# Exchanging four quadrants' maxima by transfers within SBUF instead of a small matrix product

## The chip, the cores and the metric

The kernel runs on one core of a Trainium2 chip. The metric is the device time of one execution, in microseconds (us); less is better. The time before is 823.92 us, the median of three runs.

## The reference

Two attention steps share one set of 32 inducing points, and a maxout layer follows:

```python
B, N, m, C = (4, 12544, 32, 128)      # scale = 1 / sqrt(C)

def mab(q, kv):
    s = scale * (q @ kv.transpose(0, 2, 1))
    s = s - s.max(-1, keepdims=True)
    a = np.exp(s)
    a /= a.sum(-1, keepdims=True) + 1e-09
    return a @ kv
h = mab(I, x)            # 32 inducing points attend to 12544 tokens
out = mab(x, h)          # each token attends to the 32 results

h = np.maximum(np.maximum(x @ w1, x @ w2), x @ w3)   # x: out, 50176 x 128; 768 wide
return h @ w_out
```

All of it is in float32. The softmax of the first step runs over all tokens of a batch, so a maximum over 12544 scores is needed for each of the 32 inducing points; the kernel keeps a running one and rescales.

## The kernel before

**Tiling.** A batch has 98 tiles of 128 tokens. They form seven groups: group 0 with two tiles, groups 1 to 6 with 16. A group of 16 tiles is cut into four chunks of 512 tokens, group 0 is one chunk of 256; that makes 25 chunks in a batch and 100 in all. The 768 hidden columns are six pieces of 128.

**Two phases at once.** Phase 1 of a batch is the first attention, inducing points over tokens. Phase 2 is the second attention and the maxout layer for every token, and is most of the work. Phase 1 of batch 0 runs alone at the start (`phase1_first`). Phase 1 of batches 1 to 3 is woven into phase 2 of the batch before.

**Slots.** Phase 2 is a list of 600 slots, one for each chunk and piece. `advance` issues for slot s: the product pu of the next slot (line 669), pv of this one (675), the relu ru of pu on ScalarE (684), the high part hi of the slot before (691, ScalarE), its low part lo (699 on GpSimd, or 705 on VectorE), and the maximum h of pv and ru on VectorE (702). Six slots later `stage2` multiplies hi and lo by w_out into acc (727 to 729; line 726 once in a chunk). The banks of pu, pv and acc come in pairs, so pu of slot s+2 waits until ru of slot s has read its bank, and pv of slot s+2 waits for h of slot s. `finish` copies a chunk's acc on ScalarE and stores it through SyncE's queue (744, 745).

**The order is written out by hand** for all five engines: each engine runs its instructions in the order in which the code issues them. `main` goes through the slots and, after `advance`, calls what the table `plan` holds for that slot; `at(s, f, ...)` enters a call. A window is 24 slots, one group of 16 tiles; its first slot is s0. Bursts of products for phase 1 and for the scores of phase 2 stand at s0 + 2 and s0 + 15.

**The softmax of phase 1 for one group** (`softmax1`), where the change lies. `attend_products` (282) writes the scores to a PSUM bank in four quadrants: partition 32 q + m holds inducing point m over quarter q of the group's tokens. So a maximum along a partition is that of one quarter only, and the four quadrants must be joined:

- `attend_max` (292, VectorE): the negative maximum mq of each partition.
- `attend_column` (299, ScalarE): md, mq put in the column of its quadrant of four columns.
- `attend_spread` (306, TensorE): a product of md with the constant sel, which gives every partition the values of all four quadrants of its inducing point.
- `attend_least` (312, or 315 and 316, VectorE): the least of the four, and of the running one in the batch's later groups, into mneg.
- `attend_weights` (322, ScalarE): the exponential a with that bias, and its sums. `attend_scale` (365): the factor al for the groups before.
- `attend_transpose` (336, VectorE), then in a later burst `attend_sums` (346, TensorE) and `attend_add` (382).

The argument `wait` of `softmax1` delays the steps after md; for groups 2 and 3 of a batch it is LATE.

**SyncE's queue (SP)** issues nearly all transfers, in program order: for each chunk four copies within SBUF that lay out its probabilities pT (654), 32 partitions each; the output stores; for each group two loads of 1 MB, the tokens xg (100, `load_tokens`) and the channels xT (111, `load_channels`); and at a batch's end 16 copies for its weights us (570). An instruction of SP that waits holds back all behind it. A transfer also waits until the eighth transfer before it has landed, because eight semaphores are used in turn.

Of the kernel before, what the change touches and what calls it, by code (L numbers as in the profile page):

```python
# [8 lines left out]
F32 = mybir.dt.float32  # L9
# [4 lines left out]
ALU = mybir.AluOpType  # L14
AX = mybir.AxisListType
# [10 lines left out]
def kernel(ctx, tc, x, xt, ind_t, w1, w2, w3, w_out, out):  # L26
    nc = tc.nc
    B, N, C = x.shape
    M = ind_t.shape[1]
    DF = w1.shape[1]  # L30
    P = 128
    NT = N // P
    NJ = DF // P
    NQ = P // M
# [18 lines left out]
    ORDER = "a a a a b a a b 0 c d m b a b a b a p d b 1 c s b b b s S m b q 2 c s 3 c s d s s d s"  # L53
    STEPS2 = (3, 5, 7, 8, 9, 10, 11, 13, 14, 15)
    scale = 1.0 / float(C) ** 0.5
    LATE = 12
    LOWVEC = (23, 0, 15, 18)
    LOWLAST = (23, 0, 9, 15, 18)
    UW = 2 * DF + C
# [5 lines left out]
    while t0 < NT:  # L65
        nt = NT % GT if t0 == 0 and NT % GT else GT
        assert nt == GT or nt <= NQ
        g = dict(t0=t0, nt=nt, at=t0 * P)
        groups.append(g)
        t0 += nt  # L70
    NG = len(groups)

    const = ctx.enter_context(tc.tile_pool(name="const", bufs=1))
    xp = ctx.enter_context(tc.tile_pool(name="xp", bufs=2))
    xtp = ctx.enter_context(tc.tile_pool(name="xtp", bufs=7))
    wk = ctx.enter_context(tc.tile_pool(name="wk", bufs=2))
    bp = ctx.enter_context(tc.tile_pool(name="bp", bufs=2))
    hp = ctx.enter_context(tc.tile_pool(name="hp"))
    op = ctx.enter_context(tc.tile_pool(name="op", bufs=2))
# [45 lines left out]
    def first_loads():  # L125
# [13 lines left out]
        out=sel[:, :M], in_=ident.rearrange("p (q m) -> p m q", m=M), axis=AX.X, op=ALU.add  # L139
    )  # L140
    nc.vector.tensor_copy(
        out=sel[:, M:].rearrange("p (q m) -> p q m", m=M),
        in_=sel[:, :M].unsqueeze(1).to_broadcast([P, NQ - 1, M]),
# [94 lines left out]
    state = {}  # L238

    def start_batch(b):  # L240
        st = state[b] = {"xT": {}, "xg": {}, "a": {}, "s": {}}
        st["mneg"] = bp.tile([P, NG], F32, name="mneg", tag="mneg")
        st["lst"] = bp.tile([P, NG], F32, name="lst", tag="lst")
        if b == 0:
            st["hg"] = const.tile([P, NG, C], F32, name="hg")
        else:
            st["hs"] = bp.tile([P, C], F32, name="hs", tag="hs")
# [39 lines left out]
    def attend_max(b, gi):  # L287

        w = groups[gi]["nt"] * M
        st = state[b]  # L290
        mq = wk.tile([P, 1], F32, name="mq", tag="mq")
        nc.vector.tensor_reduce(out=mq, in_=st["a"][gi][:, :w], axis=AX.X, op=ALU.max, negate=True)
        st["mq"] = mq

# [13 lines left out]
    def attend_least(b, gi):  # L308
        st = state[b]
        new, mp = st["mneg"][:, gi : gi + 1], st["mp"]  # L310
        if b == 0 or gi == 0:
            nc.vector.tensor_reduce(out=new, in_=mp[:, :NQ], axis=AX.X, op=ALU.min)
        else:

            nc.vector.tensor_reduce(out=mp[:, NQ : NQ + 1], in_=mp[:, :NQ], axis=AX.X, op=ALU.min)
            nc.vector.tensor_tensor(out=new, in0=mp[:, NQ : NQ + 1], in1=st["mneg"][:, gi - 1 : gi], op=ALU.min)

    def attend_weights(b, gi):
        w = groups[gi]["nt"] * M
        st = state[b]  # L320
        a = wk.tile([P, 512], F32, name="a", tag="a")
        nc.scalar.activation(
            out=a[:, :w],
            in_=st["a"][gi][:, :w],
            func=AF.Exp,
            bias=st["mneg"][:, gi : gi + 1],
            accum_out=st["lst"][:, gi : gi + 1],
        )
        st["a"][gi] = a
# [32 lines left out]
    def attend_scale(b, gi):  # L362
        st = state[b]
        st["al"] = wk.tile([P, 1], F32, name="al", tag="al")
        nc.scalar.activation(
            out=st["al"],
            in_=st["mneg"][:, gi - 1 : gi],
            func=AF.Exp,
            bias=st["mneg"][:, gi : gi + 1],
            scale=-1.0,  # L370
        )

# [25 lines left out]
    def phase1_first():  # L398
# [19 lines left out]
        half(1, 0)  # L418
        attend_spread(0, bank_o[0])
        attend_least(0, 0)  # L420
        half(1, 8)
        work(WORK[0])
# [347 lines left out]
    def at(s, f, *args):  # L770
        plan[s].append((f, args))

    def softmax2(b, gi, *when):

        gen = []

        def step():
            if not gen:
                gen.append(scores_steps(b, gi))
            next(gen[0], None)  # L780

        for s in when:
            at(s, step)

    def softmax1(b, gi, s, wait=0):

        at(s + 2, attend_max, b, gi)
        at(s + 3, attend_column, b)
        at(s + 6 + wait, attend_spread, b)
        at(s + 7 + wait, attend_least, b, gi)  # L790
        at(s + 8 + wait, attend_weights, b, gi)
        if gi > 0:
            at(s + 9 + wait, attend_scale, b, gi)
        at(s + 10 + wait, attend_transpose, b, gi)

    def burst(s, *what):

        for f, *args in what:
            at(s, f, *args)

    for b in range(B):
        base = b * per_batch + short
        n = b + 1
        for g in range(1, NG):
            s0 = base + (g - 1) * WIN
            first, second = [], []
            if g + 1 < NG:

                if n == B:

                    if g % 2:
                        first += [(scores_products, b, k, bank_a[k % 2]) for k in (g + 1, g + 2) if k < NG]
                elif b > 0 or g > 1:
                    first.append((scores_products, b, g + 1, bank_a[0]))
                softmax2(b, g + 1, *(s0 + i for i in STEPS2))
            if n < B:

                if g == 1:
                    if n == 1:
                        at(s0 + 1, load_tokens, 1, 4)  # L820
                    at(s0 + 4, load_channels, n, 2)
                    first.append((attend_products, n, 0, bank_a[1]))
                    softmax1(n, 0, s0 + 2)
                    second += [(attend_products, n, 1, bank_a[1]), (attend_sums, n, 0)]
                    at(s0 + 16, attend_add, n, 0)
                    softmax1(n, 1, s0 + 15)
                    at(s0 + 16, load_tokens, n + 1, 0)
                    at(s0 + 20, load_channels, n, 3)
                elif g < NG - 2:
                    first += [(attend_products, n, g, bank_a[1]), (attend_sums, n, g - 1)]  # L830
                    at(s0 + 3, attend_add, n, g - 1)
                    softmax1(n, g, s0 + 2, 0 if g == NG - 3 else LATE)
                    at(s0 + 4, load_channels, n, g + 2)
                    more = g + 3
                    if more < NG:
                        at(s0 + 5, load_tokens, n, more)
                    else:
                        at(s0 + 5, load_tokens, n + 1, more - NG + 1)
                    if g == NG - 3:
                        second += [(attend_products, n, g + 1, bank_a[1]), (attend_sums, n, g)]  # L840
                        at(s0 + 16, attend_add, n, g)
                        softmax1(n, g + 1, s0 + 15)
                        at(s0 + 16, load_tokens, n + 1, 2)
                elif g == NG - 2:
                    first += [(attend_products, n, g + 1, bank_a[1]), (attend_sums, n, g)]
                    at(s0 + 3, attend_add, n, g)
                    softmax1(n, g + 1, s0 + 2)
                    at(s0 + 5, load_tokens, n + 1, 3)
                    second.append((attend_sums, n, g + 1))
                    at(s0 + 16, load_tokens, n + 1, 4)  # L850
                    at(s0 + 16, attend_add, n, g + 1)
                    at(s0 + 18, add_quadrants, ("state", n), bank_a[1])
                    at(s0 + 18, total_sums, ("state", n), bank_a[0])
                    at(s0 + 19, invert_total, ("state", n))
                    at(s0 + 19, combine_states, ("state", n), 1)
                    at(s0 + 21, combine_products, ("state", n), bank_a[0])
                    at(s0 + 22, combine_high, ("state", n))
                    at(s0 + 23, combine_low, ("state", n))
                    for r in range(NQ):
                        at(s0 + 25 + 3 * r, combine_rows, ("state", n), r)  # L860
                else:
                    first += [(scores_products, n, 1, bank_a[0]), (scores_products, n, 0, bank_a[1])]
                    softmax2(n, 1, *(s0 + i for i in STEPS2))
                    softmax2(n, 0, *(s0 + i for i in (4, 6, 8, 9, 10, 11, 12, 13, 14, 15)))
                    if n + 1 < B:
                        at(s0 + 18, start_batch, n + 1)
                        at(s0 + 18, load_channels, n + 1, 0)
                        at(s0 + 18, load_channels, n + 1, 1)
            burst(s0 + 2, *first)
            burst(s0 + 15, *second)  # L870
# [25 lines left out]
    with tc.manual_schedule(engines=MANUAL):  # L896
        phase1_first()
        st = state[0]
# [9 lines left out]
        for step in ORDER.split():  # L908
# [10 lines left out]
            elif step == "m":  # L919
                more = len(st["up"])  # L920
# [67 lines left out]
```

## Time and profile before

| what | value |
|---|---|
| runs | 823.32, 823.92, 826.77 us; median 823.92 us |
| span of the profiled execution | 821.3 us; the median lies 2.6 us above it |
| busy: TensorE, ScalarE, GpSimd, VectorE | 98%, 91%, 79%, 76% |
| granted clock of TensorE | 1.000 over the span |
| DMA | 102.51 MB, mean 125 GB/s |

A row of a group of instructions reads: line of the kernel, engine, operation, output <- inputs, shapes, number of instructions, then busy time and mean length. A row of a timeline reads: start, length, engine, line, operation, number, and in brackets the engine's idle time before it with what ended that. PE is TensorE, DVE is VectorE, ACT is ScalarE, SPq is SyncE's queue. A matmul of float32 data takes two passes, each with a record of its own (the spread: 56 records for 28 products). Matmuls overlap, so the distance between starts tells what one costs.

### The profile page before, as it was taken

Reading aid. Unit: us, or ns where it says so; the run is one execution under the profiler, and the core shown is the slowest. Engines: PE = TensorE matmul, PEld = TensorE weight load, DVE = VectorE, ACT = ScalarE, POOL = GpSimd, SP = SyncE. Lnnn points to the kernel's source line nnn. Section 1 sums busy time; section 2 is a strip of 40 time slices with the busy share of each in tenths; the row PEclk is TensorE's granted clock in tenths of the full one; section 3 lists DMA queues with packets and bytes.
Section 4 is the critical chain, followed back from the end, with each engine's and each line's share of the span. In section 5 each row is a group of like instructions: output and inputs, shape, how many; then the busy total and the mean of one; then the engine's idle time right before and its main releaser. Section 6 shows DMA issues by size and latency. Waiting matters only on the chain.

```text
span 821.3 us, 14725 instructions
## 1 busy us (share of the span) xinstructions
PE 809.0 (98%) x4604; PEld 634.0 (77%) x4604; DVE 627.4 (76%) x1090; ACT 743.5 (91%) x1558; POOL 650.1 (79%) x521
## 2 busy tenths in 40 slices
PE   7989999999999999999999999999999999999998
PEld 5757778778788787777778777877778788787886
DVE  4977778777787687787786877877778788778864
ACT  5779889898899898898999988989889899899996
POOL 1269779778799697787888977977879889888887
PEclk9999999999999999999999999999999999999999
DMA  8844534433443544344334352431223222222221
GB/s 325 310 137 151 188 88 161 161 120 107 136 139 121 154 154 162 84 162 159 110 106 142 116 205 83 159 119 58 63 80 89 71 78 77 65 81 76 63 78 52
DMA packets 44206, 102.51 MB, mean 125 GB/s; under 512 B 9568, under 2 KB 13536, under 8 KB 38880
## 3 DMA queue, kind: packets, MB, share of 16 engines
q1 hardware_dynamic: 43984, 101.44, 38.5%
q8 instruction: 37, 0.61, 0.3%
q14 instruction: 41, 0.34, 0.1%
q10 hardware_dynamic: 144, 0.13, 0.0%
HBM read 48.12 MB, written 25.69 MB: 90 GB/s over the span
## 4 chain that ended last, share of the span: by engine, by line
PE 95%; DMA 2%; DVE 1%; SPq 1%; ACT 1%; issue 0%; ACTq 0%; DVEq 0%
PE acc L727 17%; PE pv L675 16%; PE acc L728 16%; PE acc L729 16%; PE pu L669 16%; PE aux L585 3%; PE acc L726 3%; PE acc L346 3%; PE aux L282 2%; DMA xg<-in_x_dram 2%; PE acc L306 0%; PE pu L272 0%; SPq L100 0%; PE pv L272 0%; PE aux L551 0%; DMA pT<-pl 0%
## 5 line engine op out<-in xcount | busy, mean ns | idle before, releaser
L699 POOL TENSOR_TENSOR lo<-h,hi 128x512 fp32r<-128x512 f32 (+1 forms) x502 | 634.9, 1295 | 129.8 <-ACT hi L691 84.0
L702 DVE TENSOR_TENSOR h<-pv,ru 128x512 f32<-128x512 f32 (+1 forms) x600 | 404.2, 675 | 167.8 <-PE pv L675 81.2
L684 ACT ACTIVATE ru<-pu 128x512 f32<-128x512 f32 (+1 forms) x600 | 375.3, 626 | 52.6 <-PE pu L669 49.7
L691 ACT CAST hi<-h 128x512 fp32r<-128x512 f32 (+1 forms) x600 | 386.4, 644 | 0.4 <-DVE h L702 0.3
L727 PE MATMUL acc<-hi,wo_hi 128*128 128x512 f32 (+1 forms) x600 | 236.9, 395 | 0.0
L675 PE MATMUL pv<-pT,us 128*128 128x512 f32 (+1 forms) x600 | 232.1, 387 | 0.3 <-DVE h L702 0.3
L669 PE MATMUL pu<-pT,us 128*128 128x512 f32 (+1 forms) x600 | 231.5, 386 | 0.4 <-DMA pT<-pl 0.4
L728 PE MATMUL acc<-hi,wo_lo 128*128 128x512 f32 (+1 forms) x600 | 231.5, 386 | 0.0
L729 PE MATMUL acc<-lo,wo_hi 128*128 128x512 f32 (+1 forms) x600 | 231.2, 385 | 0.0
L727 PEld LDWEIGHTS acc<-hi,wo_hi 128*128 128x128 f32 x600 | 112.7, 188 | 30.0 <-issue 8.7
L675 PEld LDWEIGHTS pv<-pT,us 128*128 128x128 f32 x600 | 112.6, 188 | 24.2 <-DVE h L702 1.6
L669 PEld LDWEIGHTS pu<-pT,us 128*128 128x128 f32 x600 | 112.6, 188 | 23.9 <-DMA pT<-pl 0.6
L729 PEld LDWEIGHTS acc<-lo,wo_hi 128*128 128x128 f32 x600 | 112.7, 188 | 23.0
L728 PEld LDWEIGHTS acc<-hi,wo_lo 128*128 128x128 f32 x600 | 112.8, 188 | 21.1
L705 DVE TENSOR_TENSOR lo<-h,hi 128x512 fp32r<-128x512 f32 x98 | 71.3, 727 | 0.7 <-ACT hi L691 0.7
L744 ACT COPY o<-acc 128x512 f32<-128x512 f32 (+1 forms) x99 | 61.1, 617 | 0.0
L726 PE MATMUL acc<-pT,us 128*128 128x512 f32 (+1 forms) x100 | 38.7, 387 | 0.0
L346 PEld LDWEIGHTS acc<-xg,aT 128*32 128x32 f32 x768 | 21.1, 110 | 11.4 <-issue 6.8
L282 PE MATMUL aux<-xT,iT 128*32 128x512 f32 x192 | 25.3, 598 | 1.6 <-ACT xT L274 1.6
L346 PE MATMUL acc<-xg,aT 128*32 128x128 f32 x768 | 25.6, 274 | 0.0
L585 PE MATMUL aux<-xT,hT 128*32 128x512 f32 x192 | 25.1, 603 | 0.0
L192 POOL TENSOR_TENSOR rest<-rest,t 128x768 f32<-128x768 f32 x3 | 5.5, 1824 | 24.3 <-DVE rest L184 24.3
(119 smaller groups left out, 445.4 us busy)
## 6 DMA issues: line engine op xcount, KB each, us to landing
out_dram<-o SPq DMA_DIRECT2D x95, 256.0 KB, 2.0
xg<-in_x_dram SPq DMA_DIRECT2D x23, 1024.0 KB, 6.9
xT<-in_xt_dram SPq DMA_DIRECT2D x18, 1024.0 KB, 5.2
pT<-ph SPq DMA_DIRECT2D x192, 64.0 KB, 2.0
pT<-pl SPq DMA_DIRECT2D x192, 64.0 KB, 2.0
raw<-in_w_dram SPq DMA_DIRECT2D x3, 768.0 KB, 9.5
us<-uh SPq DMA_DIRECT2D x24, 52.0 KB, 1.9
us<-ul SPq DMA_DIRECT2D x24, 52.0 KB, 1.9
```

The costliest lines, as they stand in the source:

```text
L346: nc.tensor.matmul(out=hps[q * M : (q + 1) * M, :C], lhsT=aT[:, t * M : (t + 1) * M], rhs=xg[:, t, :], start=(t < NQ), stop=(t + NQ >= nt),)
L669: nc.tensor.matmul(out=pu[:, :w], lhsT=state[c.b]["us"][:, 2 * j * P : (2 * j + 1) * P], rhs=c.pT[:, :w], start=True, stop=True)
L675: nc.tensor.matmul(out=pv[:, : d.w], lhsT=state[d.b]["us"][:, (2 * j + 1) * P : (2 * j + 2) * P], rhs=d.pT[:, : d.w], start=True, stop=True,)
L684: nc.scalar.activation(out=ru[:, :w], in_=pu[:, :w], func=AF.Relu)
L691: nc.scalar.copy(out=hi[:, : c.w], in_=h[:, : c.w])
L699: nc.gpsimd.tensor_sub(**args)
L702: nc.vector.tensor_max(out=h[:, : d.w], in0=pv[:, : d.w], in1=relus.pop(s)[:, : d.w])
L705: nc.vector.tensor_sub(**low)
L726: nc.tensor.matmul(out=c.acc[:, :w], lhsT=us[:, 2 * DF :], rhs=c.pT[:, :w], start=True, stop=False)
L727: nc.tensor.matmul(out=c.acc[:, :w], lhsT=wo_hi[:, j, :], rhs=c.hh[j][:, :w], start=False, stop=False)
L728: nc.tensor.matmul(out=c.acc[:, :w], lhsT=wo_lo[:, j, :], rhs=c.hh[j][:, :w], start=False, stop=False)
L729: nc.tensor.matmul(out=c.acc[:, :w], lhsT=wo_hi[:, j, :], rhs=c.hl[j][:, :w], start=False, stop=(j == NJ - 1))
```

## The change

In batches 1 to 3 the steps md, spread and least are replaced. The tile mx has, for each group, five words in a partition: the partition's own negative maximum, three places for those of the other quadrants, and the running least of the groups before. Six transfers within SBUF, issued by SP, fill the three places: for a rotation by 32 k partitions (k = 1, 2, 3) one transfer moves the upper part and one the lower. One reduction over four words, or five from group 1 on, then gives the least. Batch 0 keeps the product.

The table of slots changes with it: the exchange stands in the slot of the maximum; the least comes one slot later than before and so does the exponential, while the transpose stays. LATE falls from 12 to 8, so that for groups 2 and 3 the steps from the least on come three or four slots earlier. Most of the big loads move five slots later (two from s0 + 20 to s0 + 22, and the load of group 4's tokens at s0 + 16 stays).

```diff
-    LATE = 12
+    LATE = 8
...
-        st["mneg"] = bp.tile([P, NG], F32, name="mneg", tag="mneg")
+        if b == 0:
+            st["mneg"] = const.tile([P, NG], F32, name="mneg")
+        else:
+            st["mx"] = bp.tile([P, NG + 1, NQ + 1], F32, name="mx5", tag="mx5")
...
-        mq = wk.tile([P, 1], F32, name="mq", tag="mq")
+        mq = wk.tile([P, 1], F32, name="mq", tag="mq") if b == 0 else st["mx"][:, gi, 0:1]
...
-        if b == 0 or gi == 0:
-            nc.vector.tensor_reduce(out=new, in_=mp[:, :NQ], axis=AX.X, op=ALU.min)
-        else:
-
-            nc.vector.tensor_reduce(out=mp[:, NQ : NQ + 1], in_=mp[:, :NQ], axis=AX.X, op=ALU.min)
-            nc.vector.tensor_tensor(out=new, in0=mp[:, NQ : NQ + 1], in1=st["mneg"][:, gi - 1 : gi], op=ALU.min)
+        nc.vector.tensor_reduce(out=new, in_=mp[:, :NQ], axis=AX.X, op=ALU.min)
+
+    def exchange_maxima(b, gi):
+
+        st = state[b]
+        for k in range(1, NQ):
+            for to, at_, n in ((0, k * M, P - k * M), (P - k * M, 0, k * M)):
+                nc.sync.dma_start(out=st["mx"][to : to + n, gi, k : k + 1], in_=st["mx"][at_ : at_ + n, gi, 0:1])
+
+    def running_least(b, gi):
+        st = state[b]
+        nc.vector.tensor_reduce(
+            out=least(st, gi), in_=st["mx"][:, gi, : NQ + (gi > 0)], axis=AX.X, op=ALU.min
+        )
+
+    def least(st, gi):
+        return st["mx"][:, gi + 1, NQ : NQ + 1] if "mx" in st else st["mneg"][:, gi : gi + 1]
...
-            bias=st["mneg"][:, gi : gi + 1],
+            bias=least(st, gi),
...
         at(s + 2, attend_max, b, gi)
-        at(s + 3, attend_column, b)
-        at(s + 6 + wait, attend_spread, b)
-        at(s + 7 + wait, attend_least, b, gi)
-        at(s + 8 + wait, attend_weights, b, gi)
+        at(s + 2, exchange_maxima, b, gi)
+        at(s + 8 + wait, running_least, b, gi)
+        at(s + 9 + wait, attend_weights, b, gi)
...
-                    at(s0 + 4, load_channels, n, g + 2)
+                    at(s0 + 9, load_channels, n, g + 2)
...
-                        at(s0 + 5, load_tokens, n, more)
+                        at(s0 + 10, load_tokens, n, more)
```

Three places show what moves, all at group 1 of batch 2. The line numbers of the changed kernel are 14 higher there for TensorE's and SP's old steps. On SP, between two output stores, before:

```order
L745 DMA out_dram<-o 128x512
L654 DMA pT<-ph 32x512 x2
L654 DMA pT<-pl 32x512 x2
L100 DMA xgs<-in_x_dram 128x256
L745 DMA out_dram<-o 128x512
L111 DMA xT<-in_xt_dram 128x2048
L654 DMA pT<-ph 32x512 x2
L654 DMA pT<-pl 32x512 x2
```

And in the changed kernel, with the exchange on line 321:

```order
L759 DMA out_dram<-o 128x512
L668 DMA pT<-ph 32x512 x2
L668 DMA pT<-pl 32x512 x2
L321 DMA mx_3154<-mx_3154 96x1
L321 DMA mx_3154<-mx_3154 32x1
L321 DMA mx_3154<-mx_3154 64x1 x2
L321 DMA mx_3154<-mx_3154 32x1
L321 DMA mx_3154<-mx_3154 96x1
L759 DMA out_dram<-o 128x512
L100 DMA xgs<-in_x_dram 128x256
L668 DMA pT<-ph 32x512 x2
L668 DMA pT<-pl 32x512 x2
```

The six transfers stand behind a chunk's four pT and ahead of the next output store; the load xgs went behind that store, and xT (not shown) behind the next chunk's pT. On VectorE, from the maximum (292) to the step after the least (315, 316), before:

```order
L292 TENSOR_REDUCE mq<-aux_80 128x1
L702 TENSOR_TENSOR h<-pv_83,ru 128x512
L702 TENSOR_TENSOR h<-pv_84,ru 128x512
L702 TENSOR_TENSOR h<-pv_83,ru 128x512
L705 TENSOR_TENSOR lo<-h,hi 128x512
L702 TENSOR_TENSOR h<-pv_84,ru 128x512
L702 TENSOR_TENSOR h<-pv_83,ru 128x512
L315 TENSOR_REDUCE acc_85<-acc_85 128x1
L316 TENSOR_TENSOR mneg<-acc_85,mneg 128x1
L702 TENSOR_TENSOR h<-pv_84,ru 128x512
```

And in the changed kernel (295 is the maximum, 716 the h, 719 the lo, 325 the new reduction):

```order
L295 TENSOR_REDUCE mx_5758<-aux_80 128x1
L716 TENSOR_TENSOR h<-pv_83,ru 128x512
L716 TENSOR_TENSOR h<-pv_84,ru 128x512
L716 TENSOR_TENSOR h<-pv_83,ru 128x512
L719 TENSOR_TENSOR lo<-h,hi 128x512
L716 TENSOR_TENSOR h<-pv_84,ru 128x512
L716 TENSOR_TENSOR h<-pv_83,ru 128x512
L716 TENSOR_TENSOR h<-pv_84,ru 128x512
L325 TENSOR_REDUCE mx_5758<-mx_5758 128x1
L716 TENSOR_TENSOR h<-pv_83,ru 128x512
```

Six h stand between the maximum and the least now, five before, and one small instruction has gone. On TensorE, around the spread (306), before:

```order
L669 MATMUL pu_81<-pT,us 128x512
L675 MATMUL pv_84<-pT,us 128x512
L306 MATMUL acc_86<-md,sel 128x4
L727 MATMUL acc_85<-hi,wo_hi 128x512
L728 MATMUL acc_85<-hi,wo_lo 128x512
```

And in the changed kernel:

```order
L683 MATMUL pu_81<-pT,us 128x512
L689 MATMUL pv_84<-pT,us 128x512
L741 MATMUL acc_85<-hi,wo_hi 128x512
L742 MATMUL acc_85<-hi,wo_lo 128x512
L743 MATMUL acc_85<-lo,wo_hi 128x512
```

The spread is gone and nothing stands in its place; the second stage follows pv at once.

More of the change, by code (lines that the diff above doesn't have):

```diff
@@ L366, in attend_scale @@
             out=st["al"],
-            in_=st["mneg"][:, gi - 1 : gi],
+            in_=least(st, gi - 1),
             func=AF.Exp,
-            bias=st["mneg"][:, gi : gi + 1],
+            bias=least(st, gi),
             scale=-1.0,
@@ L820 @@
                         at(s0 + 1, load_tokens, 1, 4)
-                    at(s0 + 4, load_channels, n, 2)
+                    at(s0 + 9, load_channels, n, 2)
                     first.append((attend_products, n, 0, bank_a[1]))
@@ L826 @@
                     softmax1(n, 1, s0 + 15)
-                    at(s0 + 16, load_tokens, n + 1, 0)
-                    at(s0 + 20, load_channels, n, 3)
+                    at(s0 + 21, load_tokens, n + 1, 0)
+                    at(s0 + 22, load_channels, n, 3)
                 elif g < NG - 2:
@@ L832 @@
                     softmax1(n, g, s0 + 2, 0 if g == NG - 3 else LATE)
-                    at(s0 + 4, load_channels, n, g + 2)
+                    at(s0 + 9, load_channels, n, g + 2)
                     more = g + 3
                     if more < NG:
-                        at(s0 + 5, load_tokens, n, more)
+                        at(s0 + 10, load_tokens, n, more)
                     else:
-                        at(s0 + 5, load_tokens, n + 1, more - NG + 1)
+                        at(s0 + 10, load_tokens, n + 1, more - NG + 1)
                     if g == NG - 3:
@@ L842 @@
                         softmax1(n, g + 1, s0 + 15)
-                        at(s0 + 16, load_tokens, n + 1, 2)
+                        at(s0 + 21, load_tokens, n + 1, 2)
                 elif g == NG - 2:
@@ L847 @@
                     softmax1(n, g + 1, s0 + 2)
-                    at(s0 + 5, load_tokens, n + 1, 3)
+                    at(s0 + 10, load_tokens, n + 1, 3)
                     second.append((attend_sums, n, g + 1))
```

## The prediction

> **What bounds the kernel now.** I read the page first: the busy shares and the chain of work that ended last.
>
> ```profile
> span 821.3 us, 14725 instructions
> PE 809.0 (98%) x4604; PEld 634.0 (77%) x4604; DVE 627.4 (76%) x1090; ACT 743.5 (91%) x1558; POOL 650.1 (79%) x521
> ...
> PE 95%; DMA 2%; DVE 1%; SPq 1%; ACT 1%; issue 0%; ACTq 0%; DVEq 0%
> ```
>
> TensorE (PE) is busy for 98% of the span and makes 95% of the chain. A busy PE alone proves little, so I asked next what PE waited for. In the answer of the waits for PE alone, only these two rows belong to the repeated work of the slots:
>
> ```profile
> PE pu L669 <- DMA pT<-pl: 0.4, 1, 0.4
> PE pv L675 <- DVE h L702: 0.3, 1, 0.3
> ```
>
> Each is one wait, together 0.7 us of 821.3. So in batches 1 to 3, where the change lies, the time is the sum of the starting distances of PE's instructions. Whatever leaves PE's list shortens the run by its distance, and whatever leaves ScalarE (ACT), VectorE (DVE) or SyncE's queue (SP) shortens nothing. The change can lose only by making PE wait where it doesn't now.
>
> **The product that goes.** The spread product (line 306) stands in the answer for its source line with first and last start, and then in PE's timeline at one place, group 1 of batch 2:
>
> ```profile
> L306 PE MATMUL acc<-md,sel x56: 167/252/273, 6.8 to 584.2; 128*128 128x4 f32 x56
> ```
>
> ```profile
> 274.60 0.39 PE L675 MATMUL pv<-pT,us 128*128 128x512 f32 x1
> ...
> 275.73 0.39 PE L675 MATMUL pv<-pT,us 128*128 128x512 f32 x1
> 275.96 0.28 PE L306 MATMUL acc<-md,sel 128*128 128x4 f32 x2
> 276.10 0.48 PE L727 MATMUL acc<-hi,wo_hi 128*128 128x512 f32 x1
> ...
> 277.11 0.39 PE L675 MATMUL pv<-pT,us 128*128 128x512 f32 x1
> ...
> 280.74 0.39 PE L675 MATMUL pv<-pT,us 128*128 128x512 f32 x1
> ```
>
> 56 records are 28 products of two passes each: seven groups in each of four batches. Batch 0 keeps its seven, so 21 go. Their price isn't their length (matmuls overlap) but what they add to the distance between neighbours. A slot without a spread goes from pv to pv in 275.73 - 274.60 = 1.13 us; the slot with it takes 277.11 - 275.73 = 1.38 us. Price: 0.25 us each. Sum: 21 x 0.25 = 5.2 us off PE's list. A lower bound would be 0, if another limit took over at each place; more than 5.2 us I exclude, since besides it PE has only those 0.7 us of waits to lose.
>
> **What ACT and DVE lose.** ACT loses 21 column scalings (md), DVE loses the pair L315/L316 in 18 groups and one reduction in three, and gets one reduction over four or five words in 21. Neither engine is waited for now, so I cost this at nothing. It matters only as relief, below.
>
> **The exchange that comes.** In its place SP issues six transfers for each group, 126 in all, behind a new wait for the maximum (mq on DVE). The trace has no transfer of one word per partition. The nearest rows are transfers within SBUF of 32 partitions (pT, line 654), and the smallest load (iT, 128 bytes in each partition):
>
> ```profile
> 268.54 1.15 SPq L654 DMA_DIRECT2D pT<-ph  x2
> 269.78 1.17 SPq L654 DMA_DIRECT2D pT<-pl  x2
> 271.05 0.53 SPq L100 DMA_DIRECT2D xgs<-in_x_dram  x1
> 273.93 0.34 SPq L745 DMA_DIRECT2D out_dram<-o  x1
> ```
>
> ```profile
> L654 SPq DMA_DIRECT2D pT<-pl x192: 507/588/1537, 51.7 to 796.6; - x192
> ...
> DMA to landing us min/median/max: 1.9/2.0/6.2
> ```
>
> ```profile
> xg<-in_x_dram SPq DMA_DIRECT2D x23, 1024.0 KB, 6.9
> xT<-in_xt_dram SPq DMA_DIRECT2D x18, 1024.0 KB, 5.2
> ...
> iT<-in_ind_t_dram SPq DMA_DIRECT2D x1, 16.0 KB, 1.8
> ```
>
> Issue: two pT take 269.78 - 268.54 = 1.24 us, 0.62 each. The bounds are 0.34 (an output store) and 1.54 (the longest pT). I take 0.62, since the exchange too goes from SBUF to SBUF. Landing: bounds 1.8 (iT) and 6.2 (the worst pT, behind big loads); I take 2.0. Then the exchange is complete 0.1 (SP takes up work) + 5 x 0.62 + 2.0 = 5.2 us after the maximum. A gain from it is excluded, since nothing waits for it less than for the product.
>
> When is it needed? The DVE timeline of the same place:
>
> ```profile
> 272.70 0.68 DVE L292 TENSOR_REDUCE mq<-aux 128x1 f32<-128x512 f32 x1
> 273.30 1.34 DVE L702 TENSOR_TENSOR h<-pv,ru 128x512 f32<-128x512 f32 x2
> 275.13 0.69 DVE L702 TENSOR_TENSOR h<-pv,ru 128x512 f32<-128x512 f32 x1 [0.48 <-ACT hi L691]
> ...
> 278.20 0.16 DVE L315 TENSOR_REDUCE acc<-acc 128x1 f32<-128x4 f32 x1
> ...
> 278.77 0.69 DVE L702 TENSOR_TENSOR h<-pv,ru 128x512 f32<-128x512 f32 x1 [0.21 <-PE pv L675]
> ```
>
> The maximum is ready at 272.70 + 0.68 = 273.38. In the new order of DVE six h stand between it and the new reduction; the sixth is the one at 278.77, done at 279.46. So the exchange has 6.1 us for 5.2: it lands 0.9 us before DVE asks. SP is free at 273.38: its row at 271.05 ends at 271.58, and the store at 273.93 goes behind the exchange. If it were late, DVE would stand at the reduction with all later h behind it. PE needs the h that ended at 279.46 for pv two slots on, at 280.74: another 1.28 us of cover. PE waits only from 2.2 us beyond 5.2. Fifteen of the 21 exchanges have six h of room. The six of groups 2 and 3 have fourteen, although LATE falls from 12 to 8, and can't matter.
>
> **What is queued behind SP's new wait.** Behind the six transfers stand a store, the loads moved here, and the next chunk's four pT: each up to 6 x 0.62 = 3.7 us later. SP has the room:
>
> ```profile
> SPq L745 <- ACT o L744: 325.9, 80, 6.6
> ```
>
> That is 325.9 us in which SP only waited for output copies. A chunk's pT is requested seven slots, about 8 us, ahead of its first product; 3.7 us late with 2.0 us of landing still fits. If that cover were gone, PE would wait at pu (line 669). The loads of 1 MB moved by five slots land in 5.2 and 6.9 us and are used more than a window later: nothing. Without that move they would stand in front of the exchange and share its engines; five slots later they have seven slots to land before the window's second exchange.
>
> The Trainium skill speaks against this change: its page "DMA: Bandwidth & Descriptors", section "Rules for kernel authors", says that many small transfers should be one big one and that two transfers to disjoint halves serialize. The pT rows here disagree as far as they go: transfers 0.62 us apart each land in 2.0 us, so their fixed times overlap. What the page's "Specifications" say on writes under 512 bytes (a read-modify-write) no trace here shows.
>
> **ACT is the second limit.** The exponential a moves one slot nearer to the transpose that waits for it. And ACT works without a pause in some windows, as its timeline and PE's show at group 4 of batch 2:
>
> ```profile
> 352.16 0.30 ACT L299 ACTIVATE md<-quad,mq 128x4 f32<-128x4 f32 x1
> 352.36 0.59 ACT L684 ACTIVATE ru<-pu 128x512 f32<-128x512 f32 x1
> ...
> 361.84 0.68 ACT L684 ACTIVATE ru<-pu 128x512 f32<-128x512 f32 x1
> ```
>
> ```profile
> 362.77 0.39 PE L669 MATMUL pu<-pT,us 128*128 128x512 f32 x1
> ```
>
> The ru at 361.84 ends at 362.52, and the pu at 362.77 overwrites its bank: 0.25 us of margin. With the spread gone PE comes there 0.25 us sooner; with md gone ACT comes 352.36 - 352.16 = 0.20 us sooner. The margin falls to 0.20 us and holds. The same list of ACT work stands ahead of the burst after groups 4 and 6 of each of three batches, six places; I allow 0.05 us at each, 0.3 us.
>
> **Sum.** 821.3 - 5.2 + 0.3 = 816.4 us of span. The median of 823.92 lies 2.6 us above the span; that stays. 816.4 + 2.6 = 819.0 us.
>
> **Rivals.**
>
> A, ACT takes over. If ACT isn't sooner at those places, because the exponential now sits in a fuller slot, PE gives back its 0.25 us at six places: 1.5 us, 820.2. If half of every group's gain goes, 2.6 us are left: 821.3. For it: the margin of 0.25 us and ACT at 91%. Against: ACT's work falls, and PE's bursts refill the margin. Chance 0.24.
>
> B, the exchange is late (slower). At the new reduction each early exchange completes 0.1 + 5p + 2.0 us after the maximum, for an issue time p; PE pays what exceeds 6.1 + 1.28 = 7.4 us, fifteen times. That begins at p = 1.05 and outweighs the 5.2 us from p = 1.12. At twice my row, p = 1.24, PE pays 0.9 x 15 = 13.5 us: 832. At the longest pT, 1.54, it pays 2.4 x 15 = 36 us: 855. For it: one word per partition is untried here. Against: 192 pT with a median of 0.59. Chance 0.08.
>
> C, the transfers land one after another. Six landings of 2.0 us are 12.1 us after the maximum, 4.7 us beyond 7.4, fifteen times: 70 us, about 889. The Trainium skill's rule on serializing transfers, in the page named above, would have it so. The overlapping pT are against it. Chance 0.02.
>
> D, the change doesn't do what it says: the 0.25 us come back as waits at the same places, for DVE or pT. The time stays at 823 to 824. Against: the margins of 0.9 + 1.28 us. Chance 0.06.
>
> **How the numbers follow.** My own case has 0.60: 818.2 to 819.8, its unknowns being ACT's 0.3 us and the scatter of a median. A measurement of this kernel can tell about 0.5%, 4.1 us, from no change; 819.8 is that border. Faster by more is my case, 0.60. Within 0.5% are A and D, 0.30. Slower are B and C, 0.10. The range takes in my case and A, 0.84 together: 818.0 to 822.4.
>
> **What would show it.** Right: 14 records of the spread instead of 56 (batch 0 alone), 1.13 us from pv to pv across the old places, exchange issues near 0.6 us landing near 2 us, and PE's list of waits as short as before. A would show as waits of PE pu for ACT ru shortly before the bursts; B and C as waits of DVE's new reduction for a DMA, above 1.3 us, followed by waits of PE for h; a broken pT cover as waits of PE pu for pT. I am wrong if PE's waits after the first 60 us exceed 1.5 us, or if the span falls although PE waits.

## The result, and the profile after

| | median, us | range, us | runs |
|---|---|---|---|
| changed kernel | 819.14 | 818.25 to 823.59 | 18 |
| kernel before, beside it on the same chip | 822.77 | 821.84 to 826.77 | 18 |

The ratio is 0.995, 95% interval 0.9939 to 0.9961: faster by 3.2 to 5.0 us. The profiled execution took 818.58 us, its span is 816.8 us, and the granted clock is 1.000. The forecast was 819.0 us, and a span of 816.4.

The page of the changed kernel, first the span and the busy shares, then the chain:

```profile
span 816.8 us, 14868 instructions
PE 804.4 (98%) x4562; PEld 628.4 (77%) x4562; DVE 624.8 (76%) x1072; ACT 740.4 (91%) x1537; POOL 651.0 (80%) x521
...
PE 94%; DMA 3%; ACT 1%; DVE 1%; SPq 1%; issue 0%; DVEq 0%
```

TensorE's busy time fell by 809.0 - 804.4 = 4.6 us, nearly what the span lost (4.5 us), with 4604 - 4562 = 42 fewer passes of products. It bounds the kernel as before. The spread's line now:

```profile
L309 PE MATMUL acc<-md,sel x14: 172/253/273, 6.4 to 35.3; 128*128 128x4 f32 x14
```

14 passes are batch 0's seven products; the other 21 are gone. The place of the prediction, PE's timeline at group 1 of batch 2:

```profile
275.10 0.39 PE L689 MATMUL pv<-pT,us 128*128 128x512 f32 x1
...
276.24 0.39 PE L689 MATMUL pv<-pT,us 128*128 128x512 f32 x1
276.46 0.39 PE L741 MATMUL acc<-hi,wo_hi 128*128 128x512 f32 x1
...
277.37 0.39 PE L689 MATMUL pv<-pT,us 128*128 128x512 f32 x1
```

From pv to pv it is 1.14 and then 1.13 us, where the second distance was 1.38 us. Did the time come back as waits? Of PE's waits only these two belong to the slots, the same two with the same sizes as before:

```profile
PE pu L683 <- DMA pT<-pl: 0.4, 1, 0.4
PE pv L689 <- DVE h L716: 0.3, 1, 0.3
```

The exchange by its source line, issue times in ns as least, median and most, then the landings:

```profile
L321 SPq DMA_DIRECT2D mx<-mx x126: 493/591/1396, 60.2 to 580.0; - x126
...
DMA to landing us min/median/max: 1.7/1.7/3.3
```

The issue is that of pT (0.59 us), the landing 0.3 us under pT's. From issue to issue it is 0.63 us. Set beside the ends of the maxima, most of the 21 exchanges are complete 4.90 to 4.95 us after their maximum, and VectorE asks at 5.6 to 6.25 us in the fifteen places with little room. Four took 5.5 us or longer. The worst took 6.71 us, at the predicted place itself, where one issue and one landing were slow. SP's and then VectorE's timeline there:

```profile
271.71 3.93 SPq L321 DMA_DIRECT2D mx<-mx  x6
```

```profile
271.00 0.68 DVE L295 TENSOR_REDUCE mx<-aux 128x1 f32<-128x512 f32 x1
...
276.76 0.69 DVE L716 TENSOR_TENSOR h<-pv,ru 128x512 f32<-128x512 f32 x1 [0.48 <-PE pv L689]
278.47 0.16 DVE L325 TENSOR_REDUCE mx<-mx 128x1 f32<-128x5 f32 x1 [1.01 <-DMA mx<-mx]
```

The maximum ends at 271.68 and VectorE has to wait 1.01 us at the least. That is its only wait for an exchange in the run, and PE doesn't wait after it: 1.01 is less than the further cover of 1.28 us.

The four slow exchanges aren't chance: in a second trace of this kernel (run 8) the same four take 5.4 to 6.7 us. Beside SP's transfers the DMA view of the window 271 to 279 shows packets of two other queues, whose kind the page calls instruction (packets, MB, share of 16 engines):

```profile
q8 instruction: 1, 0.02, 0.8%
q14 instruction: 2, 0.02, 0.7%
```

They are packets of 16 and 8 KB. Seven traces have this exchange and these slots of the loads (this one and those of runs 1, 7, 8 and 9), with 147 exchanges. During 86 no such packet moves, and each of these is complete 4.87 to 4.92 us after SP begins. All 35 that take longer, up to 7.3 us, have one; 26 have one and aren't longer. So it is likely that these packets hold the transfers up, but no run moves them to show it.

**Where the 4.5 us are, slot by slot.** The start of pu in each of the 600 slots can be set side by side in the two traces; where the difference changes, a slot has gained or lost. At each of the 21 old places of the spread it changes by 0.24 us (0.237 in all but rounding): 21 x 0.237 = 5.0 us gained. Seven places lose. Six slots behind bursts lose 0.07 to 0.10 each, 0.5 us together. Slots 53 and 54 (group 2 of batch 1) lose 0.38. Sum 5.0 - 0.5 - 0.4 = 4.1 us. The other 0.5 us of the span was gained before the first slot, in the start that the change doesn't touch. In the thirteen traces of these kernels the first slot starts between 47.8 and 50.8 us, so such a difference says nothing. None of the seven losses stands in the list of waits, which has only idle time of PE: a product that is held while the one before it still runs shows in the distance of the starts alone.

ScalarE's timeline at slots 52 and 53, and PE's:

```profile
110.12 0.75 ACT L336 ACTIVATE a<-aux,mx 128x512 f32<-128x512 f32 x1
110.70 0.26 ACT L336 ACTIVATION_READ_ACCUMULATOR a<-aux,mx 128x1 f32 x1
110.79 0.34 ACT L379 ACTIVATE al<-mx 128x1 f32<-128x1 f32 x1
110.97 0.65 ACT L698 ACTIVATE ru<-pu 128x512 f32<-128x512 f32 x1
```

```profile
110.28 0.39 PE L683 MATMUL pu<-pT,us 128*128 128x512 f32 x1
...
111.67 0.50 PE L683 MATMUL pu<-pT,us 128*128 128x512 f32 x1
```

The ru stands behind the exponential, its sums and al, and ends at 111.62. The pu that overwrites its bank starts at 111.67, 1.39 us after the last pu instead of 1.13. With LATE 12 these steps came in another slot.

### The profile page after: what moved, and what is told of

It reads as the page before. It is cut to its first block, busy times and chain, and to the rows that moved or that the text cites. A ratio compares the mean times of both kernels' runs of the same rounds, so it can differ in the third digit from the quotient of the medians.

```text
span 816.8 us, 14868 instructions
## 1 busy us (share of the span) xinstructions
PE 804.4 (98%) x4562; PEld 628.4 (77%) x4562; DVE 624.8 (76%) x1072; ACT 740.4 (91%) x1537; POOL 651.0 (80%) x521
## 4 chain that ended last, share of the span: by engine, by line
PE 94%; DMA 3%; ACT 1%; DVE 1%; SPq 1%; issue 0%; DVEq 0%
PE acc L741 17%; PE pu L683 16%; PE pv L689 16%; PE acc L742 16%; PE acc L743 16%; PE aux L599 3%; PE acc L740 3%; PE acc L360 3%; PE aux L285 2%; DMA xg<-in_x_dram 2%; DMA pT<-pl 1%; ACT ru L698 0%; PE pu L275 0%; SPq L100 0%; ACT hi L705 0%; PE pv L275 0%
```

## The experiments

The theory: the gain is the product's distance on PE, bought with an exchange that is hidden behind two covers, VectorE's and SP's. Each run was compared with the kernel before on the same chip.

**1. The product put back into the changed kernel**, as an idle one that nobody reads.

```diff
+    def idle_spread():
+        nc.tensor.matmul(out=spare[0][:, :NQ], lhsT=sel, rhs=quad, start=True, stop=True)
...
+        at(s + 6 + wait, idle_spread)
```

> The changed kernel, and in each of the 21 groups a product of the spread's size (sel by a constant of four columns, into the same spare bank) stands where the spread stood; nobody reads it and it waits for no engine. Theory (the gain is the product's distance on TensorE): about 0.24 us come back at each of 21 places, and the waits for ScalarE that the changed kernel has before some bursts vanish, so the time is that of the kernel before, 822.3 to 823.5. Rival (the gain came from less work on ScalarE and VectorE, or from the moved loads): it stays near 819.

Measured: 824.59 us (823.2 to 826.42), ratio 1.0009 (0.9997 to 1.0022). Its page, and its PE at the known place:

```profile
span 821.4 us, 14952 instructions
PE 809.6 (99%) x4604; PEld 633.8 (77%) x4604; DVE 621.9 (76%) x1072; ACT 741.4 (90%) x1537; POOL 651.3 (79%) x521
```

```profile
275.72 0.39 PE L692 MATMUL pv<-pT,us 128*128 128x512 f32 x1
275.94 0.28 PE L330 MATMUL acc<-quad,sel 128*128 128x4 f32 x2
...
277.09 0.39 PE L692 MATMUL pv<-pT,us 128*128 128x512 f32 x1
```

1.37 us from pv to pv. With the exchange, the new slots and ACT's lighter list all in place, the whole gain goes with the product, and the six losses behind bursts vanish as expected. It comes out 1.1 us above the expected range: against the trace of before it loses 1.0 us at slots 53 to 55, where group 2's steps now stand, and the product with them.

**2. Only the new slots of the loads, and LATE 8, in the kernel before.** Product kept, no exchange.

```diff
-    LATE = 12
+    LATE = 8
...
-                    at(s0 + 4, load_channels, n, g + 2)
+                    at(s0 + 9, load_channels, n, g + 2)
```

(and the other loads as in the change; from s0 + 20 to s0 + 22 it is one load in each of three batches, not two in all)

> The kernel before with only the changed table: loads five slots later and LATE 8; the product, md and the two-step least stay. Theory: no transfer was waited for and SyncE's queue had idle time, so 822.3 to 823.5, as before. Rival (part of the gain is the moved loads'): 821.5 or less.

Measured: 828.7 us (827.9 to 830.42), ratio 1.0059 (1.0041 to 1.0077). Neither the theory nor the rival had it. A row of its waits of PE, and PE's timeline at one of the six places:

```profile
PE acc L726 <- DVE mneg L316: 3.8, 6, 0.7
```

```profile
307.15 0.39 PE L675 MATMUL pv<-pT,us 128*128 128x512 f32 x1
308.15 0.50 PE L726 MATMUL acc<-pT,us 128*128 128x512 f32 x1 [0.62 <-DVE mneg L316]
```

The spread's result lies in a bank of the pair that acc uses. Four slots earlier, it still waits for VectorE when the next chunk's acc wants the bank; 0.91 to 1.01 us are lost at each of six places, 5.5 us. So LATE 8 costs time with the product. The exchange, which needs no bank, makes it possible. The other 1.5 us of the longer span lie before the first slot, within what the starts differ by.

**3. The loads alone**, LATE 12.

> The kernel before with the loads in their new slots, and LATE left at 12. Theory (the moved loads bring nothing by themselves; what cost time in the run with both moves was LATE 8, which put the least behind the point where the next chunk's acc needs the spread's bank): 822.3 to 823.7, no wait of TensorE for the least. Rival (the later loads cost time by themselves): 826 or more.

Measured: 822.96 us (821.95 to 827.14), ratio 1.0008 (0.9993 to 1.0023), and no slot moved by over 0.04 us. By itself the move of the loads is worth nothing.

**4. The changed kernel with the loads where they were.** The diff is that of the change's loads, backwards.

> The changed kernel with the loads in their old slots. The prediction said that the loads would then stand in front of the exchange and share its engines: the exchanges behind a load would be complete more than 7.4 us after the maximum, TensorE would wait at three to nine places, and the time would be 821 to 830. Rival: in the table the loads of a slot stand behind that slot's exchange, except at group 1's first and at loads of the slot before the second exchange, and SyncE's queue runs ahead, so that a load is mostly landed by the time of the maximum; then the time stays at 818.7 to 819.7.

Measured: 828.99 us (826.54 to 832.82), ratio 1.0069 (1.0046 to 1.0092). The time fell into the expected range, the reason was another. VectorE has no wait for an exchange; they are complete after 4.9 to 5.6 us. PE waits for pT:

```profile
PE pu L683 <- DMA pT<-pl: 6.3, 6, 1.5
```

SP's timeline in one of these windows, of this kernel and then of the changed one:

```profile
291.76 3.72 SPq L321 DMA_DIRECT2D mx<-mx  x6
295.57 0.53 SPq L111 DMA_DIRECT2D xT<-in_xt_dram  x1
296.21 0.37 SPq L100 DMA_DIRECT2D xg<-in_x_dram  x1
...
297.14 1.27 SPq L668 DMA_DIRECT2D pT<-ph  x2
```

```profile
291.66 0.38 SPq L111 DMA_DIRECT2D xT<-in_xt_dram  x1
292.13 1.17 SPq L668 DMA_DIRECT2D pT<-ph  x2
```

The old slots put both loads behind the exchange and its wait, and so 2 MB right ahead of the next chunk's pT, which leave after 297.14. In the changed kernel one load of 1 MB stands ahead of them, and xg goes behind them. At this place PE's row shows what the second costs:

```profile
306.27 0.47 PE L683 MATMUL pu<-pT,us 128*128 128x512 f32 x1 [1.48 <-DMA pT<-pl]
```

Runs 3 and 4 together: the move of the loads is no gain of its own but a condition of the exchange, worth 7.6 us at six slots once that is there. In all, the slots of this trace take 7.8 us longer than those of the changed kernel's, and 2.3 us of its span lie before the first slot, where the loads are the same. The medians differ by 828.99 - 819.14 = 9.9 us; what makes up the rest there is open.

**5. Six more transfers ahead of each exchange**, one word per partition, into a tile that nobody reads.

```diff
+        for i in range(6):
+            nc.sync.dma_start(out=st["dum"][:, gi, i : i + 1], in_=st["mx"][:, gi, 0:1])
```

> The changed kernel with six more transfers of one word per partition, into a tile that nobody reads, issued ahead of each exchange. In the changed kernel an exchange is complete 4.9 us after the maximum; six more issues of 0.63 us make it 8.7 us. The prediction has the cover at 6.1 us until VectorE asks and 1.28 us more until TensorE waits, 7.4 us: TensorE should pay 1.3 us at each of 15 places, 20 us, so about 839 (833 to 846). Rival (the exchange is hidden anyway, since TensorE works from a deeper stock): 819 to 821.

Measured: 880.0 us (874.75 to 885.16), ratio 1.0675 (1.0639 to 1.0711). Too slow by 41 us against 839. PE's waits:

```profile
PE pv L692 <- DVE h L719: 22.9, 17, 2.2
PE pu L686 <- DMA pT<-pl: 19.1, 7, 3.8
```

The first row is the expected bill: VectorE waits 2.6 to 3.8 us at each of the fifteen exchanges with little room, and PE's waits behind them are 0.9 to 2.2 us. The second row was not in the sum. SP is held 7.5 us instead of 3.7, and in the windows of groups 2 and 3, where the exchange itself has room, pT comes late. Counted slot by slot the two take about 30 us each. The waits alone are 42 us of these. Much of the rest is the clock, which was in no sum either: its mean fell to 0.984, an estimated 879 x 0.016 = 14 us. The windows view (start:end, length, five busy times with counts, clock, DMA share, GB/s) of the window with the longest wait, 3.8 us, and then of the stretch in which that wait ends:

```profile
300.00:330.00 30.00, 24.69 (x134) 18.92 (x135) 20.09 (x35) 22.08 (x46) 19.86 (x15) 0.91 0.59 180
...
325.00:331.00 6.00, 5.24 (x12) 4.12 (x13) 2.04 (x4) 2.69 (x5) 1.83 (x2) 0.50 0.37 130
```

There the clock is at half, while PE works for 5.24 of 6.00 us: slots 199 to 201 lose 2.8 us behind the wait.

**6. Two more transfers**, else like run 5.

> Two extra one-word transfers ahead of each exchange, into words that nothing reads. By the pitch measured, 0.63 us, each exchange completes 1.26 us later, 6.2 us after the maximum instead of 4.9, and SP is held 1.26 us longer. Theory, in which both covers count separately: VectorE waits at most 0.5 us at most early exchanges, PE is covered by its further 1.28 us except where a transfer lands late, and the chunks' transfers of which the tightest had 0.8 us of margin come up to 0.5 us late in a few windows: 819 to 821 us. Rival, in which cost is proportional to the delay (six extra transfers cost 61 us): about 20 us, 839.

Measured: 823.31 us (822.37 to 827.49), ratio 1.001 (0.9995 to 1.0024); measured beside it, the changed kernel stood at 818.89. So two transfers, 1.26 us of SP's time per group, eat the whole gain: 4.4 us, less than the rival's 20 and more than my 0 to 2. VectorE waits 8.3 us in all at ten exchanges, and PE loses half a us behind two of them (slots 184 and 418). The rest is pT. The waits of DVE, then SP's and PE's timelines in this run:

```profile
DVE mx L328 <- DMA mx<-mx: 8.3, 10, 1.9
```

```profile
292.88 0.43 SPq L111 DMA_DIRECT2D xT<-in_xt_dram  x1
293.40 1.17 SPq L671 DMA_DIRECT2D pT<-ph  x2
```

```profile
301.82 0.47 PE L686 MATMUL pu<-pT,us 128*128 128x512 f32 x1 [1.60 <-DMA pT<-pl]
```

In the trace the load xT of this window lands at 300.77, 7.9 us after its issue, and the four pT behind it by 301.69. In the changed kernel the load took 5.6 us and the last pT was there at 298.48, 1.6 us before its pu. So 1.3 us of delay became 3.2. Why the load itself took 2.3 us longer stays open. Of the loss that shows slot by slot, 2.1 us are at slots 198 to 200, 0.7 at 258 and 259, 0.4 at 378 and 379, all behind late pT.

**7. The least and the exponential one slot earlier** in the changed kernel (s + 7 and s + 8), to see if five h of room would do.

> The changed kernel with the least and the exponential one slot earlier, where they stood before: five h of room, about 4.9 us, for an exchange that takes 4.9 us. Theory (VectorE may wait some tenths at the reduction, the 1.28 us behind it keep TensorE from it): 818.3 to 819.3. Rival (any lateness goes through to TensorE): 820 to 824.

Measured: 820.84 us (819.06 to 821.08), ratio 0.9967 (0.9956 to 0.9979). The waits of VectorE, then of PE:

```profile
DVE mx L325 <- DMA mx<-mx: 5.6, 6, 2.6
```

```profile
PE pv L689 <- DVE h L716: 1.2, 2, 0.9
```

The median lies in the rival's range, but not every lateness goes through. Fifteen exchanges have the smaller room, waits appear at six, and one of them, behind an exchange of 7.1 us at the place that is always slowest, costs PE 1.2 us. For PE an exchange of 4.9 us would fit five slots; what the sixth pays for is the few that take longer. The slots of this trace take 2.0 us longer than the changed kernel's; 0.5 of the rest stands at slots 48 and 49, where the changed kernel's second trace (run 8) loses it too.

**8. LATE 12 in the changed kernel.**

> The changed kernel with LATE 12 again. Theory (with the product gone no bank is held, and groups 2 and 3 have room either way): 818.7 to 819.7, as the changed kernel. Rival (LATE 8 is part of the gain): 820.5 or more.

Measured: 818.16 us (817.54 to 821.45), ratio 0.9948 (0.993 to 0.9965), 0.5 us below the expected range. The loss of 0.38 us at slots 53 and 54 is gone: PE's pu start there at 110.80 and 111.93, 1.13 us apart.

Both kernels were then run again side by side, the changed one first:

> The changed kernel itself, beside its variant with LATE 12 on the same chip. Theory: it stands where it stood, 819.1 us, and 0.4 us above the variant, because of the one wait at slots 53 and 54 that the variant does not have. Rival: the difference is only the scatter of the start-up, and the two medians lie within 0.2 us of each other.

> Theory: 0.3 to 0.5 us under the changed kernel in the same call, with no lost time at slots 53 and 54. Rival: within 0.2 us of it. Either way about 0.5% under the kernel before.

Measured: 818.89 us (818.18 to 822.18, 7 runs; ratio 0.9954, 0.9937 to 0.9971) and 818.57 us (817.65 to 819.88, 6 runs; ratio 0.9941, 0.9925 to 0.9957). The loss at slots 53 and 54 is in both traces with LATE 8 and in neither with LATE 12. The medians differ by 0.3 us in the expected direction, but the intervals overlap. The slot is shown; that the time is better isn't.

The second trace of the changed kernel shows more. From the first slot to the last its slots take 759.2 us, in the first trace 758.2, before 762.3; the two traces with LATE 12 have 757.7 and 757.6. So of one and the same kernel the gain in the slots was 4.1 us once and 3.0 once. The 1.0 us between is lost at slots 48 and 49 (0.6) and 353 and 354 (0.4). At both, ScalarE had stood shortly before: its next ph goes into a buffer that transfers of pT still had to read, and they were late. Its timeline ahead of slot 48:

```profile
104.88 0.59 ACT L645 CAST ph<-aux 128x512 fp32r<-128x512 f32 x1 [0.95 <-DMA pT<-pl]
```

In the first trace the only such wait (0.33 us) stands ahead of slots 53 and 54, the only place of groups 2 and 3 that loses there. With LATE 12 ScalarE has such a wait as well (0.41 us), and no slot loses. By these traces the loss at 53 and 54 takes both, the late pT and the exponential in that slot.

**9. al one slot later** in the changed kernel (s + 10), to take it from the full slot of the exponential.

> The changed kernel with the factor al (attend_scale) one slot later, so that it no longer stands in the exponential's slot on ScalarE. Theory (TensorE's remaining waits for ru, 0.5 us in total before six bursts and 0.4 us at group 2 of batch 1, come from ScalarE's fuller slot): the 0.4 us go and perhaps some of the 0.5, 818.3 to 819.0. Rival (they come from ScalarE's whole load between bursts): 818.8 to 819.5, the same waits.

Measured: 819.34 us (817.7 to 822.51), ratio 0.9961 (0.9948 to 0.9974): no gain. Slot 53 gets 0.11 us back, slot 184 loses 0.25 behind an exchange that took 7.3 us, and the six losses behind bursts stay. So they don't hang on the slot of al; that they come from all that ACT has to do ahead of a burst is likely, not shown.

## Why the prediction was right, and where it was not

**The product, 21 x 0.25 = 5.2 us: right.** 0.237 us each, 5.0 us. The distance read between the starts of two pv was the price. It didn't return as waits (rival D), and run 1 gives it back whole, which rules out that it came from lighter lists or moved loads.

**ACT's 0.3 us: the place right, the margin wrong.** The six losses of 0.07 to 0.10 us, 0.5 together, are at the predicted places, around the bursts. ACT's timeline and PE's at the place the prediction took for its margin:

```profile
359.35 0.65 ACT L698 ACTIVATE ru<-pu 128x512 f32<-128x512 f32 x1
```

```profile
360.07 0.49 PE L683 MATMUL pu<-pT,us 128*128 128x512 f32 x1
```

The ru ends at 360.00 and pu starts 0.07 us later, and 0.06 or 0.07 at all six places; at slot 53, where PE was plainly held, it is 0.05. So no margin is left, where 0.20 us was to hold. PE came there 0.24 us sooner, but ACT not 0.20: 0.25 - 0.24 + 0.20 would have left 0.21. That is rival A's mechanism at a third of its price, 0.5 us and not 1.5. Where ACT's 0.20 us went stays open. The 0.38 us at slots 53 and 54 were nowhere in the sum. "The six of groups 2 and 3 ... can't matter" is the step that failed there: it looked only at when the exchange is needed, while LATE 8 moves ACT's steps too. Run 8 shows it.

**The sum: 816.4 forecast, 816.8 measured, partly by luck.** In the slots the change brought 4.1 us, not 4.9 (in the second trace 3.0); the start gave 0.5 unasked. And the 2.6 us between span and median came from three runs of before; over the 18 runs beside the changed kernel its median was 822.77, 1.15 lower. Between the medians of 18 runs the gain is 822.77 - 819.14 = 3.6 us. The two errors of size, 1.3 us of gain too many and 1.15 us of level too high, nearly cancel in 819.0 against 819.14.

**The exchange: right.** 5.2 us forecast, 4.9 measured, because the landing takes 1.7 us and not 2.0; asked for at 5.6 to 6.25, forecast 6.1. The second cover of 1.28 us was needed once. The six transfers do overlap: one after another they would need 6 x 1.7 = 10 us. The Trainium skill's page "DMA: Bandwidth & Descriptors", section "Rules for kernel authors", says that two transfers to disjoint partition halves serialize since they share the engines; for transfers this small the trace disagrees, their landings overlap. The same section's advice to coalesce many small transfers holds in another coin: runs 5 and 6 show what each costs SP.

**"3.7 us late with 2.0 us of landing still fits": right in result, wrong in its margin.** It fits by 0.8 to 2.0 us at the six tightest chunks (before, by 5.7 to 6.6 at the same six), since pT doesn't land in 2.0 us behind a load of 1 MB but in 4.1 to 6.5. Nor is pu the only one that waits for pT: ScalarE's ph does too (run 8), and the prediction left that out. The 325.9 us in which SP waited for output copies said nothing on this; SP's room is not a sum but the smallest slack at one place. Its row is down to:

```profile
SPq L759 <- ACT o L758: 208.5, 67, 6.6
```

and it took only two more transfers (run 6) for the cover to be gone in some windows.

**"Without that move they would stand in front of the exchange": mostly wrong.** Most would stand behind it and ahead of the next chunk's pT (run 4). In run 4 one load does stand in front, at group 0 of a batch: the exchange there is complete after 5.3 to 5.6 us instead of 4.9, and VectorE still doesn't wait. The loads hurt the slots through pT, not through the exchange.

**What stays open:** why the big load of run 6 lands 2.3 us later, whether the packets of the instruction queues are what makes single exchanges take up to 7.3 us, and whether LATE 12 is better in time.

## What to carry to other kernels

Where an engine is busy for 98% of the span, price an instruction by the distance between its neighbours' starts and check that the work replacing it has cover. Count two covers for a transfer: the time until its reader asks, and the smallest slack of each transfer that stands behind it in the same queue, with the landing time read behind the loads that will stand there. Ask also who overwrites what a late transfer still reads. Moves that gain nothing alone may be what another part of the change stands on, so undo them in the changed kernel as well as trying them alone.

## What the hardware showed unexpectedly

- A transfer of one word in each of 32 to 96 partitions occupies SP's queue for 0.63 us, like a pT of 64 KB, and lands in 1.7 us. Single ones took up to 1.4 us to issue and 3.3 us to land. All exchanges of the changed kernel that took over 4.92 us had packets of the instruction queues, of 8 or 16 KB, beside them.
- A pT of 64 KB that stands behind a load of 1 MB lands 0.5 to 1.2 us after that load (297.75 to 298.48, the load at 297.25), which was 4.5 to 5.6 us after its issue and not 2.0.
- With PE waiting often, the granted clock went below one: 0.984 over the span of run 5, 0.91 in the 30 us around its longest wait of 3.8 us, and 0.50 from 325 to 331 us, right behind that wait; over the changed kernel's span it was 1.000.
